# Sparse attention with a feed-forward block on one core: the first two tiles as a unit with separate up projections and a shared down projection

## Chip, cores and metric

The kernel runs on one core of one Trainium2 chip. The metric is the device time of one execution in microseconds (us). The kernel before has a median of 783.55 us over 3 runs.

## What is computed

For 4 batches, 8 heads, 768 positions and head size 64, attention runs with a mask over blocks of 32 positions; the 512 features of each position then go through a normalised two-layer feed-forward block (512 to 2048 to 512) with a residual:

```python
scores = np.matmul(q, k.transpose(0, 1, 3, 2)) / np.sqrt(D)
mask = np.abs(blk_i - blk_j) <= 1
mask = mask | (blk_i == 0) | (blk_j == 0) | (blk_i == 23) | (blk_j == 23)
for qb in range(24):
    for kb in sampled_blocks[qb]:          # three sampled blocks a row
        mask[qb*32:(qb+1)*32, kb*32:(kb+1)*32] = True
x = softmax(np.where(mask, scores, -1e9)) @ v    # heads side by side: (4, 768, 512)
xn = (x - mu) / np.sqrt(var + 1e-06) * g_ln
out = x + np.maximum(xn @ w_ch1, 0.0) @ w_ch2
```

## The kernel before

**Tiles, visits and jobs.** The 3072 positions are 24 tiles of 128, six a batch (`TORDER`). The attention of a tile is done in visits: two for an ordinary tile (jobs of kind N), five for the tile that holds the first and last blocks (kinds H and D). A job loads the keys and values that its visits share: on SyncE's (SP's) queue one large key load, twelve small ones of sampled blocks and the values, on GpSimd's (POOL's) queue gathers of sampled values. Two rooms for keys (`ks_s`) and two for values (`vs_s`) alternate, so a job's values wait until the visits two jobs back are through.

**A visit** passes from engine to engine: `scores` (L196; PE writes `ps`), `biggest` (L236; VectorE, DVE, writes `st`), `softmax` (L249; ScalarE, ACT, writes `p`), `turn` (L257; PE transposes into `pt`, ACT copies to SBUF), `attn_v` (L267; PE writes `pv`), `evict` (L300; DVE divides into `x`). Values of a visit come one step (`LAG`) after its scores. After the last visit of a tile `norm_a` (L334) makes the normalised fp16 halves `xh` (ACT) and `xl` (POOL), and `norm_b` (L347) transposes both with DMAs from SP's queue into `xth` and `xtl`.

**The feed-forward part** (`ffn`, L351) works on units. Before, the units are tile 0 alone, then pairs (1, 2), (3, 4) and so on, and tile 23 alone. The up projection makes, for each of 16 slices of 128 hidden features, 12 matmuls (three products of fp16 halves by four slices of the 512 features), with 128 columns for one tile and 256 for a pair; four slices of one tile, or two of a pair, fill a PSUM bank `pu`. ACT's relu (L377) makes the high half `hh`, DVE (L378) the low half `hl`. The down projection of a tile (`pd`, L392) is 48 matmuls of 512 columns; DVE adds the residual (L398) and POOL's queue stores it.

**The weights** come as 64-bit numbers and are split on the chip during the first steps. `split_w` (L418): three DVE operations (L421, L423, L425) rebuild a float, ACT makes the high half, and the low half is made by POOL for w1 (L435) and by DVE for w2 (`low_w2`, L444). w1 has eight pieces, two a step in steps 0 to 3; w2 has sixteen, four a step in steps 4 to 7, loaded on POOL's queue into four raw rooms. `con1` and `con2` are the rooms where the float stands. The raw rooms `raw2[0]` and `raw2[1]` are the second halves of `hh_s` and `hl_s`, which a pair needs and a single tile doesn't.

**What sets the order.** The program writes each engine's instructions in order of a loop over steps (L551); engines take their own in order and wait for each other by semaphores. In a step come scores, the values of the visit before, softmax, and then a list of tasks (loads, weight splits, `turn`, norms) with matmuls of the feed-forward part put between them by a budget (L576 to L600). The budget counts planned costs (84 for a matmul of 128 columns, 109 for 256, 215 in the down projection). A unit enters the queue at step `u.at` (L528), for tile 0 step 4, when all its tiles have been normalised. Between steps the generator stops where a weight piece that it needs has not been written in an earlier step.

Of the kernel before, what the change touches and what calls it, by code (L numbers as in the profile page):

```python
# [10 lines left out]
F16 = mybir.dt.float16  # L11
# [8 lines left out]
SW1 = 16.0  # L20
# [5 lines left out]
def sparse_attention_moe(  # L26
# [50 lines left out]
    hl_s = const.tile([P, FT * 2 * P], F16, name="hl")  # L77
    ot_s = ring("ot", 2, [P, DM], F32)
    stg = ring("stg", 2, [P, 2048], F16)
    id_sb = const.tile([P, P], F32, name="id_sb")  # L80
    g_sb = const.tile([P, DM], F32, name="g_sb")
    eps = const.tile([P, 1], F32, name="eps")

    nc.scalar.add_instruction(
# [2 lines left out]
        )  # L87
    )

    samp = const.tile([P, 2 * NB * NR], I32, name="samp")  # L90
    bid = const.tile([P, NB + 1], F32, name="bid")
    si = const.tile([P, NB, NR], I32, name="si")
    sf = const.tile([P, NB, NR], F32, name="sf")
    cf = const.tile([P, NB, NR], F32, name="cf")
    tf = const.tile([P, NB, NR], F32, name="tf")
    rf = const.tile([P, NB], F32, name="rf")
    rows = const.tile([P, NB], I32, name="rows")

# [201 lines left out]
    def evict(vi):  # L300
        n = 2 if vi.kind == "D" else 4
        u = vi.pv[:, 0 : n * 65].rearrange("p (h e) -> p h e", e=65)
        if vi.kind == "D":
            half = sm.tile([P, 2, 65], F32, tag="half", name=f"half{vi.i}")
# [44 lines left out]
        nc.sync.dma_start_transpose(out=xtl_s[t.u.i % 2][:, :, s], in_=xl_s[t.n % 2])  # L349

    def ffn(u):  # L351
        n = len(u.tiles) * P
        xth, xtl = xth_s[u.i % 2], xtl_s[u.i % 2]
        hh = hh_s[:, 0 : FT * n].rearrange("p (f n) -> p f n", n=n)
        hl = hl_s[:, 0 : FT * n].rearrange("p (f n) -> p f n", n=n)
        step = 512 // n
        c1 = 109 if n == 256 else 84
        for f in range(0, FT, step):
            while any((1, x // 2) not in split for x in range(f, f + step)):
                yield -1  # L360
            ph = ps_f.tile([P, 512], F32, tag="pf", name=f"pu{u.i}_{f}")
            for j in range(step):
                fs = slice((f + j) * P, (f + j + 1) * P)
                m = 0
                for w, x in ((w1h, xth), (w1l, xth), (w1h, xtl)):
                    for ct in range(CT):
                        nc.tensor.matmul(ph[:, j * n : (j + 1) * n], w[:, ct, fs], x[:, ct, 0:n],  # L367
                                         start=m == 0, stop=m == 3 * CT - 1,
                                         skip_group_check=True)
                        m += 1  # L370
                        if m < 3 * CT:
                            yield c1
                if j < step - 1:
                    yield c1
            dh = hh[:, f : f + step, :].rearrange("p f n -> p (f n)")
            dl = hl[:, f : f + step, :].rearrange("p f n -> p (f n)")
            nc.scalar.activation(dh, ph, AF.Relu)  # L377
            nc.vector.scalar_tensor_tensor(out=dl, in0=ph, scalar=0.0, in1=dh,  # L378
                                           op0=ALU.max, op1=ALU.subtract)
            if f + step == FT:  # L380
                u.up_done = True
            yield c1
        for t in u.tiles:

            ts = slice(t.pos * P, (t.pos + 1) * P)
            po = ps_f.tile([P, 512], F32, tag="pf", name=f"pd{t.n}")
            m = 0
            for f in range(FT):
                while split.get((2, f), s) >= s:
                    yield -1  # L390
                for x, w in ((hh, w2h), (hl, w2h), (hh, w2l)):
                    nc.tensor.matmul(po, x[:, f, ts], w[:, f, :], start=m == 0,  # L392
                                     stop=m == 3 * FT - 1)
                    m += 1
                    if m < 3 * FT:
                        yield 215
            ot = ot_s[t.n % 2]
            nc.vector.scalar_tensor_tensor(out=ot, in0=po, scalar=1.0 / (SW1 * SW2), in1=t.x,  # L398
                                           op0=ALU.mult, op1=ALU.add)
            nc.gpsimd.dma_start(out[t.b, t.t], ot)  # L400
            t.done = True
            yield 215

    split = {}
    late = [x[:, FT * P :] for x in (hh_s, hl_s)]
    w2f, w2g = (x.rearrange("p f e -> p (f e)") for x in (w2h, w2l))
    raw1 = [w2f[:, 0:4096], w2f[:, 4096:8192], w2g[:, 0:4096], w2g[:, 4096:8192]]
    con1 = [stg[0], stg[1], late[0], late[1]]
    raw2 = [late[0], late[1], stg[0], stg[1]]
    con2 = [x.bitcast(F16) for x in ot_s]  # L410

    def load_w1(i, dma):
# [47 lines left out]
                                         done=False, ready=False, normed=None, spread=None))  # L460
    n = 0
    while n < len(tiles):
        k = 1 if n == 0 or n == len(tiles) - 1 else 2
        u = SimpleNamespace(i=len(units), tiles=tiles[n : n + k], up_done=False, gen=None)
        for pos, t in enumerate(u.tiles):
            t.pos, t.u = pos, u
        units.append(u)
        n += k
# [56 lines left out]

    queue, nextu, s = [], 0, 0
    for u in units:
        u.at = max(FFN0, u.tiles[-1].visits[-1].i + LAG + 2)  # L528

    def run(amount):  # L530
        while queue and (amount > 0 or queue[0].left <= 0):
# [19 lines left out]
    while s < NV + LAG + 2 or queue or nextu < len(units):  # L551
# [102 lines left out]
```

## Time and profile before

| | us |
|---|---|
| median of 3 runs (783.39 to 784.59) | 783.55 |
| the profiled execution | 778.71 |
| its span, first to last instruction | 776.9 |
| PE busy / DVE busy / ACT busy / POOL busy in the span | 703.0 / 324.6 / 272.2 / 190.2 |
| PE busy from 143.70 to 204.00 (60.30 long) | 60.30 |
| mean granted clock of PE | 0.961 |

PE is the engine for matrix products, DVE and ACT work on elements, POOL also issues DMAs, SP only issues DMAs. Times in the text are counted from the first instruction of the profiled execution. A matmul's busy time overlaps that of the next; what one costs in a stream is the distance between starts. Tile names in a trace come without their numbers; a word ahead of the rows says which one it is.

### The profile page before, as it was taken

To read this page: it belongs to the slowest core of one execution; us is meant where nothing else is said; L and a number is where in the kernel's file an instruction comes from. 1 tells how busy PE (TensorE), PEld (TensorE's weight loads), DVE (VectorE), ACT (ScalarE), POOL (GpSimd) and SP (SyncE) were. 2 spreads that over 40 slices of the span, in tenths; PEclk is the share of its full clock that TensorE was granted. 3 is DMA by queue.
4 is the path that set the end of the run, shared out by engine and by line. 5 is a ranking of instruction groups with operands and counts; after the bars stand their busy time and mean duration, and the time that the engine had idled before them with its cause. 6 is when DMAs were issued, how large, how long until landed. Compare 5 with 4: busy or idle time off the path is not lost.

```text
span 776.9 us, 21816 instructions
## 1 busy us (share of the span) xinstructions
PE 703.0 (90%) x9344; PEld 475.4 (61%) x9344; DVE 324.6 (42%) x658; ACT 272.2 (35%) x561; POOL 190.2 (24%) x220
## 2 busy tenths in 40 slices
PE   0566475899999999999999999999999999999997
PEld 0234452675775774875875856765856857757764
DVE  2488889443351332443432323444331433432211
ACT  0357343344342332443341523344423423342200
POOL 5276414023312103113421103115221011210000
PEclk9956788899999999999999999999999999999999
DMA  8997887467948345569855437379864248531000
GB/s 329 287 321 207 285 291 211 115 181 204 258 112 206 92 145 159 150 179 246 234 156 132 129 128 211 119 180 270 215 168 131 61 151 219 148 88 27 14 29 14
DMA packets 109792, 132.16 MB, mean 170 GB/s; under 512 B 34560, under 2 KB 80896, under 8 KB 108672
## 3 DMA queue, kind: packets, MB, share of 16 engines
q1 hardware_dynamic: 96848, 83.92, 40.0%
q0 software_dynamic: 12416, 46.51, 18.2%
q8 instruction: 74, 1.21, 0.7%
q10 hardware_dynamic: 432, 0.34, 0.1%
q14 instruction: 22, 0.18, 0.1%
HBM read 118.15 MB, written 6.29 MB: 160 GB/s over the span
## 4 chain that ended last, share of the span: by engine, by line
PE 69%; issue 14%; DVE 8%; DMA 6%; POOL 1%; ACT 1%; SPq 0%; POOLq 0%; ACTq 0%; DVEq 0%
PE pu L367 27%; PE pd L392 25%; PE ps L203 6%; PE pv L274 6%; PE pt L264 5%; DMA ks<-kT 3%; DMA vs<-v 2%; DVE ot L423 1%; DVE w2l L445 1%; DVE ot L421 1%; DVE st L239 1%; DMA hl<-w 1%; DVE ot L425 1%; DMA samp<-sampled 0%; POOL xl L344 0%
## 5 line engine op out<-in xcount | busy, mean ns | idle before, releaser
L252 ACT ACTIVATE p<-ps,st 128x256 f32<-128x256 f32 (+1 forms) x208 | 85.7, 490 | 230.2 <-DVE rs L316 140.1
L367 PEld LDWEIGHTS <-w1h 128*128 128x128 f16 x1664 | 152.8, 98 | 18.6 <-issue 0.7
L392 PE MATMUL pd<-w2l,hh 128*128 128x512 f16 x384 | 146.5, 381 | 4.0 <-DVE w2l L445 4.0
L392 PE MATMUL pd<-w2h,hl 128*128 128x512 f16 x384 | 146.5, 382 | 0.0
L392 PE MATMUL pd<-w2h,hh 128*128 128x512 f16 x384 | 146.3, 381 | 0.0
L378 DVE SCALAR_TENSOR_TENSOR hl<-pu,hh 128x512 f16<-128x512 f32 x96 | 66.4, 691 | 174.1 <-ACT hh L377 173.7
L392 PEld LDWEIGHTS <-hh 128*128 128x128 f16 x768 | 74.8, 98 | 87.2 <-issue 4.3
L367 PE MATMUL pu<-xth,w1h 128*128 128x256 f16 (+1 forms) x832 | 120.4, 266 | 0.0
L367 PE MATMUL pu<-xth,w1l 128*128 128x256 f16 (+1 forms) x832 | 120.3, 266 | 0.0
L367 PE MATMUL pu<-xtl,w1h 128*128 128x256 f16 (+1 forms) x832 | 120.0, 265 | 0.0
L192 POOL DMA_INDIRECT vs<-v,rows x88 | 87.3, 992 | 88.0 <-PE pv L274 49.4
L239 DVE TENSOR_REDUCE st<-ps 128x4 f32<-128x1024 f32 (+1 forms) x60 | 69.0, 1150 | 93.7 <-PE ps L203 93.6
L203 PE MATMUL ps<-ks,q 64*32 64x256 f32 (+1 forms) x1664 | 75.7, 426 | 30.0 <-DMA ks<-kT 29.8
L377 ACT ACTIVATE hh<-pu 128x512 f16<-128x512 f32 x96 | 57.4, 598 | 118.0 <-PE pu L367 117.3
L264 PE MATMUL pt<-id_sb,p 128*128 128x128 f32 x448 | 66.8, 293 | 33.9 <-ACT p L252 33.9
L264 PEld LDWEIGHTS pt<-id_sb,p 128*128 128x128 f32 x448 | 55.0, 149 | 46.6 <-ACT p L252 40.4
L398 DVE SCALAR_TENSOR_TENSOR ot<-pd,x 128x512 f32<-128x512 f32 x24 | 16.6, 690 | 160.3 <-PE pd L392 160.3
L367 PEld LDWEIGHTS <-w1l 128*128 128x128 f16 x832 | 77.6, 98 | 8.5
L265 ACT COPY pt<-pt 128x512 f32<-128x512 f32 x120 | 61.9, 564 | 59.2 <-PE pt L264 58.5
L400 POOL DMA_DIRECT2D out<-ot x24 | 13.9, 580 | 257.1 <-DVE ot L398 257.1
L274 PEld LDWEIGHTS pv<-vs,pt 128*32 128x32 f32 x3584 | 56.4, 113 | 31.1 <-issue 23.7
L274 PE MATMUL pv<-vs,pt 128*32 128x65 f32 x3584 | 66.7, 227 | 0.7 <-ACT pt L265 0.6
(83 smaller groups left out, 414.8 us busy)
## 6 DMA issues: line engine op xcount, KB each, us to landing
ks<-kT SPq DMA_DIRECT2D x28, 768.0 KB, 5.1
ks<-kT SPq DMA_DIRECT2D x264, 64.0 KB, 4.1
vs<-v SPq DMA_DIRECT2D x20, 780.0 KB, 7.0
vs<-v SPq DMA_DIRECT2D x4, 1560.0 KB, 8.6
q<-qT SPq DMA_DIRECT2D x24, 256.0 KB, 3.4
out<-ot POOLq DMA_DIRECT2D x24, 256.0 KB, 3.3
vs<-v SPq DMA_DIRECT2D x16, 260.0 KB, 8.6
w2h<-w POOLq DMA_DIRECT2D x4, 1024.0 KB, 7.0
```

Source lines behind the costliest of these rows:

```text
L192: nc.gpsimd.indirect_dma_start(out=vs[:, 2 * gg, :], out_offset=None, in_=src, in_offset=bass.IndirectOffsetOnAxis(ap=rows[:, i : i + 1], ...
L203: nc.tensor.matmul(ps[32 * part : 32 * part + 32, col : col + n], lhs[64 * row : 64 * row + 64], rhs[64 * row : 64 * row + 64], start=True ...
L239: nc.vector.tensor_reduce(out=st[:, 0:n], in_=seen(vi), axis=AX.X, op=ALU.max, negate=True)
L252: nc.scalar.activation(p_s[:, h * w : (h + 1) * w], seen(vi)[:, h, :], AF.Exp, bias=vi.st[:, 4 + h : 5 + h], scale=0.125)
L264: nc.tensor.transpose(pt[:, k - lo, :], p_s[:, k * P : (k + 1) * P], id_sb)
L265: nc.scalar.copy(dst[:, lo:hi, :], pt[:, 0 : hi - lo, :])
L274: nc.tensor.matmul(pv[32 * row : 32 * row + 32, 65 * col : 65 * col + 65], pt[:, ch, 32 * row : 32 * row + 32], vs[:, vv, 65 * e : 65 * e ...
L367: nc.tensor.matmul(ph[:, j * n : (j + 1) * n], w[:, ct, fs], x[:, ct, 0:n], start=m == 0, stop=m == 3 * CT - 1, skip_group_check=True)
L377: nc.scalar.activation(dh, ph, AF.Relu)
L378: nc.vector.scalar_tensor_tensor(out=dl, in0=ph, scalar=0.0, in1=dh, op0=ALU.max, op1=ALU.subtract)
L392: nc.tensor.matmul(po, x[:, f, ts], w[:, f, :], start=m == 0, stop=m == 3 * FT - 1)
L398: nc.vector.scalar_tensor_tensor(out=ot, in0=po, scalar=1.0 / (SW1 * SW2), in1=t.x, op0=ALU.mult, op1=ALU.add)
```

## The change

Tiles 0 and 1 become one unit with a mark `apart`, tile 2 a unit of its own; from tile 3 on the pairs are the same as before. A unit that is apart enters the queue at step 3 as soon as its first tile has been normalised. Its up projections run one after the other, each with 128 columns, tile 1's result in the second half of `hh_s` and `hl_s`; its down projections run side by side, 3 matmuls of the one tile and 3 of the other for each slice of hidden features. The planned cost of a matmul of 128 columns is 62 instead of 84. Since the second halves are in use sooner, w2's raw rooms 0 and 1 move: one to the last quarter of `w2l`, one to a new room `room`, in which the index of the sampled blocks is made at the start. The half results of the D visits get two fixed rooms.

```diff
+    room = const.tile([P, 2048], F16, name="room")
+    half_s = ring("half", 2, [P, 2, 65], F32)
-    samp = const.tile([P, 2 * NB * NR], I32, name="samp")
+    part = room.bitcast(I32)
+    samp = part[:, 0 : 2 * NB * NR]
+    sf, cf, tf = (part[:, (2 + k) * NB * NR : (3 + k) * NB * NR].bitcast(F32)
+                  .rearrange("p (n r) -> p n r", r=NR) for k in range(3))
-    sf = const.tile([P, NB, NR], F32, name="sf")
-    cf = const.tile([P, NB, NR], F32, name="cf")
-    tf = const.tile([P, NB, NR], F32, name="tf")
...
     def ffn(u):
-        n = len(u.tiles) * P
...
+        groups = [[x] for x in u.tiles] if u.apart else [u.tiles]
+        for k, group in enumerate(groups):
+            n = len(group) * P
+            off = 0 if len(groups) == 1 else k * FT * P
+            while any(x.spread is None or x.spread >= s for x in group):
                 yield -1
+            hh = hh_s[:, off : off + FT * n].rearrange("p (f n) -> p f n", n=n)
+            hl = hl_s[:, off : off + FT * n].rearrange("p (f n) -> p f n", n=n)
+            cols = slice(group[0].pos * P, group[0].pos * P + n)
...
-        c1 = 109 if n == 256 else 84
+            c1 = 109 if n == 256 else 62
...
-        for t in u.tiles:
+        for group in [u.tiles] if u.apart else [[x] for x in u.tiles]:
+            po = [ps_f.tile([P, 512], F32, tag="pf", name=f"pd{x.n}") for x in group]
             for f in range(FT):
+
                 while split.get((2, f), s) >= s:
                     yield -1
-                for x, w in ((hh, w2h), (hl, w2h), (hh, w2l)):
...
+                for k, x in enumerate(group):
+                    for m, (y, w) in enumerate(((x.hh, w2h), (x.hl, w2h), (x.hh, w2l))):
...
-    raw2 = [late[0], late[1], stg[0], stg[1]]
+    raw2 = [w2g[:, 6144:8192], room, stg[0], stg[1]]
...
-        k = 1 if n == 0 or n == len(tiles) - 1 else 2
+        k = 1 if n == 2 or n == len(tiles) - 1 else 2
...
-        u.at = max(FFN0, u.tiles[-1].visits[-1].i + LAG + 2)
+        u.at = FFN0 if u.apart else u.tiles[-1].visits[-1].i + LAG + 2
...
-            if any(t.spread is None or t.spread >= s for t in u.tiles):
+            if any(t.spread is None or t.spread >= s for t in u.tiles[: 1 if u.apart else 2]):
...
-            u.left = 192 * (84, 109)[len(u.tiles) - 1] + 48 * 215 * len(u.tiles)
+            half = len(u.tiles) == 1 or u.apart
+            u.left = 192 * (62 * len(u.tiles) if half else 109) + 48 * 215 * len(u.tiles)
```

What this moves on the engines shows at three places. In the rows `ps3` belongs to visit 3, `pv2` to visit 2, `pt3` to visit 3; `pu0_4` is the bank of tile 0's slices 4 to 7.

PE, from the scores of visit 3 on. Before:

```order
L203 MATMUL ps3_531<-ks1_80,q1_89 32x256 x16
L274 MATMUL pv2_551<-vs1_84,pt0_86 32x65 x32
L264 MATMUL pt3_0_592<-id_sb_110,p_85 128x128 x4
L264 MATMUL pt3_4_598<-id_sb_110,p_85 128x128 x4
L203 MATMUL ps4_620<-ks0_79,q0_88 32x256 x16
L274 MATMUL pv3_640<-vs1_84,pt1_87 32x65 x32
L367 LDWEIGHTS w1h_75
L367 MATMUL pu0_0_681<-xth0_100,w1h_75 128x128
```

Now, with the repeated pairs of weight load and matmul left out (pu0_0 has 48, and 16 of pu0_4 stand ahead of the turn of visit 3):

```order
L206 MATMUL ps3_530<-ks1_80,q1_89 32x256 x16
L277 MATMUL pv2_550<-vs1_84,pt0_86 32x65 x32
L376 LDWEIGHTS w1h_75
L376 MATMUL pu0_0_591<-xth0_100,w1h_75 128x128
...
L376 MATMUL pu0_4_655<-xth0_100,w1h_75 128x128
L267 MATMUL pt3_0_672<-id_sb_111,p_85 128x128 x4
L267 MATMUL pt3_4_678<-id_sb_111,p_85 128x128 x4
```

The first up projection has moved ahead of the turn of visit 3; the scores of visit 4 now follow 144 up matmuls, and the last 48 of tile 0 stand behind the values of visit 3.

DVE, at the same place, between the last operation on w1 and the first on w2. Before:

```order
L425 SCALAR_TENSOR_TENSOR hl_105<-w2l_78,hl_105 128x1024
L239 TENSOR_REDUCE st4_637<-ps4_620 128x4
L240 TENSOR_SCALAR st4_637<-st4_637 128x4
L316 TENSOR_SCALAR rs3_673<-pv3_640 128x4
L318 RECIPROCAL rs3_673<-rs3_673 128x4
L322 TENSOR_TENSOR x1_91<-pv3_640,rs3_673 128x256
L378 SCALAR_TENSOR_TENSOR hl_105<-pu0_0_681,hh_104 128x512
L421 TENSOR_SCALAR ot0_106<-hh_104 128x512
```

Now:

```order
L436 SCALAR_TENSOR_TENSOR hl_105<-w2l_78,hl_105 128x1024
L387 SCALAR_TENSOR_TENSOR hl_105<-pu0_0_591,hh_104 128x512
L387 SCALAR_TENSOR_TENSOR hl_105<-pu0_4_655,hh_104 128x512
L387 SCALAR_TENSOR_TENSOR hl_105<-pu0_8_720,hh_104 128x512
L242 TENSOR_REDUCE st4_789<-ps4_772 128x4
L243 TENSOR_SCALAR st4_789<-st4_789 128x4
L319 TENSOR_SCALAR rs3_825<-pv3_792 128x4
L321 RECIPROCAL rs3_825<-rs3_825 128x4
L325 TENSOR_TENSOR x1_91<-pv3_792,rs3_825 128x256
L387 SCALAR_TENSOR_TENSOR hl_105<-pu0_12_833,hh_104 128x512
L432 TENSOR_SCALAR ot0_106<-w2l_78 128x512
```

All four low halves of tile 0 stand ahead of the first operation on w2 (the last row), three of them ahead of visit 4's maximum; before, one stood there.

ACT, during the second step of w2 (`w2h` from `ot0` or `ot1` is the high part of a piece, pieces 4 to 7 here). Before:

```order
L431 ACTIVATE w2h_77<-ot0_106 128x512
L377 ACTIVATE hh_104<-pu0_4_771 128x512
L431 ACTIVATE w2h_77<-ot1_107 128x512
L265 COPY pt1_87<-pt5_0_949 128x512
L265 COPY pt1_87<-pt5_4_955 128x512
L431 ACTIVATE w2h_77<-ot0_106 128x512
L431 ACTIVATE w2h_77<-ot1_107 128x512
L377 ACTIVATE hh_104<-pu0_8_923 128x512
```

Now:

```order
L442 ACTIVATE w2h_77<-ot0_106 128x512
L386 ACTIVATE hh_104<-pu1_0_1018 128x512
L442 ACTIVATE w2h_77<-ot1_107 128x512
L268 COPY pt1_87<-pt5_0_1109 128x512
L268 COPY pt1_87<-pt5_4_1115 128x512
L386 ACTIVATE hh_104<-pu1_4_1075 128x512
L442 ACTIVATE w2h_77<-ot0_106 128x512
L442 ACTIVATE w2h_77<-ot1_107 128x512
L386 ACTIVATE hh_104<-pu1_8_1144 128x512
```

Tile 1's first bank (`pu1_0`) stands where tile 0's second stood, and a further relu (`pu1_4`) stands behind the copies of visit 5; the low halves on DVE stand in the same places between the pieces. On SP and POOL the order of loads is the same; on POOL the stores of tiles 0 and 1 now follow each other.

## Rows read from the trace of the kernel before

**Rows 1.** The page, busy tenths in 40 slices of the span (19.4 us each).
```profile
PE   0566475899999999999999999999999999999997
...
DVE  2488889443351332443432323444331433432211
```

**Rows 2.** Busy time by stretch; columns: stretch, length, busy time (instructions) of each engine, granted clock, DMA, GB/s.
```profile
94.60:99.30 4.70, 4.67 (x36) 4.52 (x37) 4.05 (x7) 2.18 (x5) 1.32 (x2) 0.51 0.55 115
...
143.70:204.00 60.30, 60.30 (x924) 40.99 (x922) 24.95 (x57) 22.64 (x49) 14.92 (x18) 1.00 0.62 169
...
304.00:404.00 100.00, 100.00 (x1440) 70.26 (x1438) 41.33 (x91) 38.14 (x84) 27.96 (x32) 1.00 0.71 196
```

**Rows 3.** Timeline of PE; columns: start, us, engine, line, operation, out<-in, size, count [idle before].
```profile
75.50 0.39 PE L367 MATMUL pu<-xth,w1l 128*128 128x128 f16 x4
...
76.84 0.39 PE L367 MATMUL pu<-xth,w1l 128*128 128x128 f16 x4
...
97.35 0.63 PE L367 MATMUL pu<-xth,w1l 128*128 128x128 f16 x4
97.78 0.63 PE L367 MATMUL pu<-xtl,w1h 128*128 128x128 f16 x4
```

**Rows 4.** Chain that ended last, in order of time; columns: start, us, what.
```profile
203.99 4.47 PE pu L367 x40
209.34 6.11 PE pu L367 x56
...
248.99 6.91 PE pd L392 x32
```

**Rows 5.** Timeline of PE, values of visit 2 and turn of visit 3.
```profile
58.37 1.12 PE L274 MATMUL pv<-vs,pt 128*32 128x65 f32 x64
66.14 1.97 PE L264 MATMUL pt<-id_sb,p 128*128 128x128 f32 x8 [6.65 <-ACT p L252]
```

**Rows 6.** Timeline of SP, transposes of tile 0; the last row: DMA issues, median us to landing.
```profile
69.70 1.30 SPq L348 DMA_TRANSPOSE xth<-xh  x1
71.10 1.20 SPq L349 DMA_TRANSPOSE xtl<-xl  x1
...
xtl<-xl SPq DMA_TRANSPOSE x24, 2.9
```

**Rows 7.** Timeline of DVE, first operation on w2.
```profile
81.27 0.46 DVE L421 TENSOR_SCALAR ot<-hh 128x512 int32<-128x512 int32 x1 [0.91 <-DMA hh<-w]
```

**Rows 8.** Timeline of ACT (three rows), then of DVE, pieces 4 to 8 of w2.
```profile
93.52 0.62 ACT L343 CAST xh<-xn 128x512 f16<-128x512 f32 x1
...
100.80 0.63 ACT L431 ACTIVATE w2h<-ot 128x512 f16<-128x512 f32 x1 [2.55 <-DVE ot L425]
101.34 1.05 ACT L265 COPY pt<-pt 128x512 f32<-128x512 f32 x2
...
98.29 0.69 DVE L378 SCALAR_TENSOR_TENSOR hl<-pu,hh 128x512 f16<-128x512 f32 x1 [0.58 <-ACT hh L377]
...
101.40 0.43 DVE L421 TENSOR_SCALAR ot<-stg 128x512 int32<-128x512 int32 x1
...
111.81 0.42 DVE L421 TENSOR_SCALAR ot<-hh 128x512 int32<-128x512 int32 x1
```

**Rows 9.** Timeline of PE, turn of visit 8.
```profile
139.63 1.54 PE L264 MATMUL pt<-id_sb,p 128*128 128x128 f32 x6 [4.60 <-ACT p L252]
```

**Rows 10.** Timeline of SP, loads for visits 13 to 16 and transposes of tiles 3 and 4.
```profile
166.33 0.33 SPq L180 DMA_DIRECT2D vs<-v  x1
...
183.43 0.42 SPq L144 DMA_DIRECT2D ks<-kT  x1
185.71 0.34 SPq L180 DMA_DIRECT2D vs<-v  x1
...
198.05 1.21 SPq L349 DMA_TRANSPOSE xtl<-xl  x1
```

**Rows 11.** The page, costliest groups: busy us, mean ns of one.
```profile
L367 PEld LDWEIGHTS <-w1h 128*128 128x128 f16 x1664 | 152.8, 98 | 18.6 <-issue 0.7
```

More of the change, by code (lines that the diff above doesn't have):

```diff
@@ L303, in evict @@
         if vi.kind == "D":
-            half = sm.tile([P, 2, 65], F32, tag="half", name=f"half{vi.i}")
+            half = half_s[vi.r % 2]
             if not vi.r:
@@ L351, in ffn @@
     def ffn(u):
-        n = len(u.tiles) * P
         xth, xtl = xth_s[u.i % 2], xtl_s[u.i % 2]
-        hh = hh_s[:, 0 : FT * n].rearrange("p (f n) -> p f n", n=n)
-        hl = hl_s[:, 0 : FT * n].rearrange("p (f n) -> p f n", n=n)
-        step = 512 // n
-        c1 = 109 if n == 256 else 84
-        for f in range(0, FT, step):
-            while any((1, x // 2) not in split for x in range(f, f + step)):
-                yield -1
[L361 to L382, printed above, removed]
@@ L383, in ffn @@
-        for t in u.tiles:
-            ts = slice(t.pos * P, (t.pos + 1) * P)
-            po = ps_f.tile([P, 512], F32, tag="pf", name=f"pd{t.n}")
-            m = 0
+        groups = [[x] for x in u.tiles] if u.apart else [u.tiles]
[3 more added lines that the diff above has]
+            while any(x.spread is None or x.spread >= s for x in group):
+                yield -1
+            hh = hh_s[:, off : off + FT * n].rearrange("p (f n) -> p f n", n=n)
+            hl = hl_s[:, off : off + FT * n].rearrange("p (f n) -> p f n", n=n)
+            cols = slice(group[0].pos * P, group[0].pos * P + n)
+            step = 512 // n
+            c1 = 109 if n == 256 else 62
+            for f in range(0, FT, step):
+                while any((1, x // 2) not in split for x in range(f, f + step)):
+                    yield -1
+                ph = ps_f.tile([P, 512], F32, tag="pf", name=f"pu{group[0].n}_{f}")
+                for j in range(step):
+                    fs = slice((f + j) * P, (f + j + 1) * P)
+                    m = 0
+                    for w, x in ((w1h, xth), (w1l, xth), (w1h, xtl)):
+                        for ct in range(CT):
+                            nc.tensor.matmul(ph[:, j * n : (j + 1) * n], w[:, ct, fs],
+                                             x[:, ct, cols], start=m == 0, stop=m == 3 * CT - 1,
+                                             skip_group_check=True)
+                            m += 1
+                            if m < 3 * CT:
+                                yield c1
+                    if j < step - 1:
+                        yield c1
+                dh = hh[:, f : f + step, :].rearrange("p f n -> p (f n)")
+                dl = hl[:, f : f + step, :].rearrange("p f n -> p (f n)")
+                nc.scalar.activation(dh, ph, AF.Relu)
+                nc.vector.scalar_tensor_tensor(out=dl, in0=ph, scalar=0.0, in1=dh,
+                                               op0=ALU.max, op1=ALU.subtract)
+                if f + step == FT and k == len(groups) - 1:
+                    u.up_done = True
+                yield c1
+            for x in group:
+                x.hh, x.hl = hh, hl
+                x.ts = slice(0, P) if u.apart else slice(x.pos * P, (x.pos + 1) * P)
@@ L390, in ffn @@
                     yield -1
-                for x, w in ((hh, w2h), (hl, w2h), (hh, w2l)):
[L392 to L395, printed above, removed]
-                        yield 215
[L397 to L402, printed above, removed]
+                for k, x in enumerate(group):
+                    for m, (y, w) in enumerate(((x.hh, w2h), (x.hl, w2h), (x.hh, w2l))):
+                        end = f == FT - 1 and m == 2
+                        nc.tensor.matmul(po[k], y[:, f, x.ts], w[:, f, :],
+                                         start=f == 0 and m == 0, stop=end)
+                        if end:
+                            ot = ot_s[x.n % 2]
+                            nc.vector.scalar_tensor_tensor(out=ot, in0=po[k],
+                                                           scalar=1.0 / (SW1 * SW2), in1=x.x,
+                                                           op0=ALU.mult, op1=ALU.add)
+                            nc.gpsimd.dma_start(out[x.b, x.t], ot)
+                            x.done = True
+                        yield 215
     split = {}
@@ L462, in sparse_attention_moe @@
     while n < len(tiles):
-        k = 1 if n == 0 or n == len(tiles) - 1 else 2
-        u = SimpleNamespace(i=len(units), tiles=tiles[n : n + k], up_done=False, gen=None)
+        k = 1 if n == 2 or n == len(tiles) - 1 else 2
+        u = SimpleNamespace(i=len(units), tiles=tiles[n : n + k], up_done=False, gen=None,
+                            apart=n == 0)
         for pos, t in enumerate(u.tiles):
```

## Prediction

> **What bounds the kernel now.** I read the page's forty slices first [rows 1]: TensorE (PE) is busy to nine tenths from the ninth slice on, and less in the eight before it; there VectorE (DVE) shows eights and a nine, in the slices three to seven, while weights are split. So the run has two stages with different limits. The busy times by stretch [rows 2] put the border: from 143.70 to 204.00 PE is busy for all of 60.30 us, and so in every stretch up to the last (304 to 404 stands for them). After about 140 us the time is PE's list of work; before it, the chain of waits runs through DVE, which turns 64-bit weights into pairs of fp16 (eight pieces of w1, sixteen of w2), and PE fills in. The order of PE's work is the same in both kernels from visit 15 on: there stands the first up projection of tiles 3 and 4, at 203.99 [rows 4]. **The change is worth what it moves that point by**, and nothing later can give it back, since PE has no idle time behind it.
>
> Two things decide it: how late the split of w2 ends, and how much PE work (or other work) is left then.
>
> **Term 1: a first stop, ahead of w2.** The first up projection (pu0_0) now stands on PE directly behind the weighted values of visit 2, which end at 58.37 + 1.12 = 59.5; before, the turn of visit 3 stood there, at 66.14 [rows 5]. pu0_0 needs the transposed halves of tile 0. SyncE (SP) issues them at 69.70 and 71.10, behind the keys, in both kernels; the second half takes 2.9 us to land [rows 6], so 74.0. Eight matmuls run on the first half, 40 wait. PE has been idle for over ten us and runs at its lower clock: after such a pause the granted clock of 94.60 to 99.30 is 0.51, that is 1.2 GHz [rows 2], and four matmuls of 128 columns take 0.43 us; at 2.4 GHz 24 take 76.84 - 75.50 = 1.34, so 0.056 each [rows 3]. 40 x 0.107 = 4.3, to 78.3. Then 16 more at 0.056 (0.9), the turn of visit 3 (8 transposes, 1.97 at the lower clock [rows 5], so 1.0), 80 up matmuls (4.5), scores and values of visits 4 and 3 (some 2.1, by the 1.12 of [rows 5]), the last 48 (2.7): 89.5. ScalarE's (ACT) relu takes about 0.63 (an equal pass over 512 columns) and DVE's low half 0.69 [rows 8]: 90.8. All of this is ahead of DVE's first piece of w2, which began at 81.27 [rows 7]. **9.5 us late**; 7.5 if the clock were full at once (40 x 0.051 less).
>
> **Term 2: a second stop, between w2's pieces 4 and 5.** There DVE now takes the low half of tile 1's first up projection; before, that of tile 0's second, long computed. Tile 1's fp16 half came 94.14 - 81.27 = 12.9 us after DVE's first w2 piece [rows 7, 8]: now 103.7. Its second transpose goes out 1.4 later and lands after 2.9 [rows 6]: 108.0; 40 matmuls at the lower clock, 112.3; relu and low half, 113.6. Piece 5 began at 98.29 + 0.69 = 98.98 [rows 8], so **14.6 late** in all. Then comes one low half more than before, ahead of piece 6. On ACT its relu stands behind the high part of piece 5 and two copies of visit 5: 101.43 - 98.98 = 2.45 after piece 5's start, plus 1.05, plus 0.63 and 0.69, makes 4.8; piece 6 began 101.40 - 98.98 = 2.4 after it [rows 8]. **2.4 more: 17.0.** With a full clock in both stops 12.9. From the higher end I take off 0.7 a stop, since PE will be some 4 us into its work when the last of the 40 run: 15.5. From piece 8 on (111.81 [rows 8]) the DVE rows are the same ones in both kernels, so the turn of visit 8, at 139.63 [rows 9], comes at 155.1.
>
> **Term 3: what PE has left then.** Before, from 139.63 to 203.99: 64.4 us. Tiles 1 and 2 went up as a pair, 192 matmuls of 256 columns at 0.109; now tile 2 alone, 192 of 128 at 0.056 [rows 3, 4]: 10.2 less. Of down matmuls 101 were left (5 and 96); now 23 and tile 2's 48, 30 fewer at 0.216 [rows 4]: 6.5 less. **64.4 - 16.7 = 47.7.** The other 192 up matmuls added (tile 1 by itself) lie in PE's idle time before 140, as do 73 down matmuls (15.8 us): from the end of tile 1's up work, at some 123 (111.6, 144 matmuls at 0.056 and two visits' 3), PE has 32 us for them and three visits' 6 us. Their cost is nothing as long as that holds.
>
> **Term 4: SP is late next.** The queue's order is unchanged, but PE now needs its loads sooner. SP is held by the values' room until visit 10 is through (the issue at 166.33), then issues that job, loads and transposes, and is ready for the next job at 183.85, 17.5 us later; from that issue (185.71) to tile 4's second transpose (198.05) are 12.3 [rows 10], and 2.9 to land. That is 32.7 us from visit 10 to the point where the up projection of tiles 3 and 4 can run. Before, PE took 203.99 - 166.33 = 37.7, and SP waited 1.9 for it. Now visit 10 ends 26.7 - 148 x 0.109 + 97 x 0.056 + 18 x 0.216 = 19.9 after the turn of visit 8 (matmuls counted in the two orders), and 52.6 would be the end of SP's chain, against PE's own 47.7. The wait is nowhere in the trace of before; its bounds are 47.7 (SP in time) and 53. I take 51.5, nearer to SP's measured length, less a microsecond because eight matmuls run ahead on the first half.
>
> **Sum.** 155.1 + 51.5 = 206.6 against 203.99: 2.6 us later. The profiled execution took 778.71, so 781.3; it lies 4.8 below the median of the runs, 783.55, and I forecast **786.2** for that. The bounds: 139.63 + 12.9 + 47.7 = 200.2 (3.8 earlier) and 139.63 + 17.0 + 53 = 209.6 (5.6 later).
>
> What costs nothing: the index's new place (the same instructions, at the start of the program, long before w2 is loaded); w2's two moved raw rooms, as all four loads still stand on POOL behind the last w1 subtraction; the two output stores, now back to back; the fixed rooms for half results.
>
> **Rivals.** *SP does not bind.* Its issues are paced by the landing of earlier loads, which may be quicker; then PE's 47.7 stands, 155.1 + 47.7 = 202.8, 1.2 earlier: no change. With the stops at 14.2 (midway to their lower bound) it is 201.5, 2.5 earlier and 781.1, **faster**. It decides at tile 4's transpose landing within 47.7 of visit 8's turn. For it speaks that SP had 1.9 us to spare; against it, that 32.7 is measured and nothing on SP is removed. Chance 0.30, a little over half of it faster.
>
> *PE falls behind under the split.* The turn of visit 6 now has 22 down matmuls ahead of it (4.8 us), and ACT's next piece of w2 stands behind its copies. By my times it is about 1.5 us late; what of that reaches DVE adds to the sum: 787.7. Chance 0.13.
>
> *Weight loads set the pace at 128 columns.* A weight load is busy for 98 ns [rows 11]; if it did not overlap, tile 2's 192 would cost 192 x 0.042 = 8.1 more, PE's 47.7 become 55.8, and the run 790.5. The rows speak against it: 24 pairs of load and matmul pass in 1.34 us [rows 3]. Chance 0.04. The Trainium skill speaks against the change here: "TensorE: Matmul & The Clock Gate", section "Back-to-back issue gap", gives about 81 ns sustained for pairs of weight load and matmul at 128 columns, and says the shorter gap of an isolated matmul leaves out the weight load. By it (an estimate from that page) tile 2 would cost 4.8 more, nearly all of it behind SP's chain, and the run about 787; this trace does not agree, with 56 ns a pair.
>
> That the down projections don't really move is excluded by the order: 73 of 96 stand ahead of visit 8's turn.
>
> **How the numbers follow.** The forecast case has 0.53; in 0.07 of that the stops come out a microsecond and a half shorter, which is no change. 0.2% is 1.6 us, about what the runs can tell (they spread over 1.2). Faster 0.16 (SP in time and short stops). Same 0.14 + 0.07 = 0.21. Slower 0.46 + 0.13 + 0.04 = 0.63. The likeliest case alone spans 784.5 to 788.5; the range runs from 779.8, the lower bound of the sum (783.55 - 3.8), to 790.5, past its upper bound (789.2) to the last rival.
>
> **What would show it.** In the profile after: DVE's first w2 operation near 91 instead of 81.27, idle before it and released by ACT's relu; a second idle time of some 5 us ahead of tile 1's first low half; visit 8's turn near 155; PE waiting for SP's loads (keys at visits 13 and 15, or a transpose) between 185 and 207, where it had no idle time before; the up projection of tiles 3 and 4 near 206.6, and equal stretches after it. If visit 8's turn comes before 153, the stops are mis-sized; if PE shows no wait for loads, term 4 falls and the result is no change or better.

## The result: 1.2% slower, and what the profile after shows

The changed kernel has a median of 792.87 us (791.93 to 793.80, 4 runs), the kernel before 783.52 in the same comparison: a ratio of 1.0117, 95% interval 1.0104 to 1.0130, 9.35 us slower. The forecast was 786.2 with a range up to 790.5. The sign was right; the time lies 2.4 us past the range.

| us | before | after | forecast |
|---|---|---|---|
| DVE, first operation on w2 | 81.27 | 90.14 | 90.8 |
| turn of visit 8 | 139.63 | 154.79 | 155.1 |
| visit 10's end (value load issued) | 166.33 | 174.43 | 175.0 |
| up projection of tiles 3 and 4 | 203.99 | 213.66 | 206.6 |
| span of the profiled execution | 776.9 | 790.2 | |

The forecast holds up to visit 10 and fails behind it. The page of the changed kernel, busy tenths in slices of 19.8 us, to be laid beside [rows 1]: PE has a four in the eighth slice (138 to 158) and a seven in the eleventh (198 to 217), where it had an eight and a nine.

```profile
PE   0464669499799999999999999999999999999997
...
DVE  2487668754233242343351423443432433442211
```

The two stops. DVE's timeline after (start, us, engine, line, operation, tiles, size, idle time and its releaser): the low half of tile 0's last bank, the first operation on w2, the low half of tile 1's first bank, piece 8.

```profile
89.53 0.69 DVE L387 SCALAR_TENSOR_TENSOR hl<-pu,hh 128x512 f16<-128x512 f32 x1 [2.98 <-ACT hh L386]
90.14 0.46 DVE L432 TENSOR_SCALAR ot<-w2l 128x512 int32<-128x512 int32 x1
...
111.30 0.69 DVE L387 SCALAR_TENSOR_TENSOR hl<-pu,hh 128x512 f16<-128x512 f32 x1 [5.07 <-ACT hh L386]
...
126.95 0.42 DVE L432 TENSOR_SCALAR ot<-w2l 128x512 int32<-128x512 int32 x1
```

PE's timeline at the same places, and the turn of visit 8:

```profile
72.06 0.59 PE L376 MATMUL pu<-xth,w1h 128*128 128x128 f16 x4 [10.61 <-DMA xth<-xh]
...
105.14 0.58 PE L376 MATMUL pu<-xth,w1h 128*128 128x128 f16 x4 [13.32 <-DMA xth<-xh]
...
154.79 1.54 PE L267 MATMUL pt<-id_sb,p 128*128 128x128 f32 x6 [9.17 <-ACT p L255]
```

PE stands for 10.61 and 13.32 us at a transpose, DVE behind it. Piece 8 is 15.14 us later than in [rows 8], the turn of visit 8 is 15.16 later than in [rows 9].

Where it went wrong. SP's timeline after: the value load behind visit 10, then the value load, the twelve key loads and the transposes of the next job, which are the rows of [rows 10].

```profile
174.43 0.33 SPq L183 DMA_DIRECT2D vs<-v  x1
...
192.17 0.45 SPq L183 DMA_DIRECT2D vs<-v  x1
...
195.87 12.38 SPq L156 DMA_DIRECT2D ks<-kT  x12
208.35 1.21 SPq L351 DMA_TRANSPOSE xth<-xh  x1
209.65 1.21 SPq L352 DMA_TRANSPOSE xtl<-xl  x1
```

From 174.43 to 192.17 are 17.74 us (17.5 forecast), but from there to the second transpose 17.48, not 12.3. The twelve key loads take 12.38; the list of SP's waits (us in total, times, longest) for 195 to 210 says why:

```profile
SPq L156 <- DMA vs<-v: 6.1, 2, 5.7
```

SP stops at the seventh key load, the eighth DMA behind the value load of 192.17, from 199.01 to 204.89, until that load has landed, 12.7 us after its issue. In the kernel before, the same list has no such row at this place: there the seventh key load went out at 193.68 without a wait, so the value load of 185.71 had landed by then, in at most 8.0 us. SP's timeline at the seventh key load, after and before:

```profile
204.89 0.33 SPq L156 DMA_DIRECT2D ks<-kT  x1
```

```profile
193.68 0.33 SPq L153 DMA_DIRECT2D ks<-kT  x1
```

PE's timeline shows what hangs on it (scores of visit 15 in three pieces, values of visit 14, up projection of tiles 3 and 4):

```profile
206.67 1.35 PE L206 MATMUL ps<-ks,q 64*32 64x256 f32 x8 [3.60 <-DMA ks<-kT]
208.26 1.06 PE L206 MATMUL ps<-ks,q 64*32 64x256 f32 x4 [0.23 <-DMA ks<-kT]
209.91 1.92 PE L206 MATMUL ps<-ks,q 64*32 64x256 f32 x20 [0.59 <-DMA ks<-kT]
211.76 1.96 PE L277 MATMUL pv<-vs,pt 128*32 128x65 f32 x64
213.66 1.03 PE L376 MATMUL pu<-xth,w1h 128*128 128x256 f16 x4
```

The waits are for keys; none for a transpose shows. Behind the 3.60 us without work the clock has fallen. Two stretches of the changed kernel (columns as in [rows 2]); the second has a granted clock of 0.50, 1.2 GHz, and the values take 1.96 us instead of 1.12 [rows 5]:

```profile
143.70:204.00 60.30, 48.62 (x815) 31.40 (x813) 32.02 (x73) 24.58 (x54) 17.42 (x20) 0.92 0.77 204
...
206.00:212.00 6.00, 4.50 (x43) 1.54 (x47) 0.13 (x1) 0.00 (x0) 0.00 (x0) 0.50 0.47 115
```

In the first of them PE was busy for all of 60.30 us before [rows 2], now for 48.62.

Why did the same load take longer? POOL's timeline, first of the kernel before, then of the changed one, with the first gather of visits 15 and 16 last:

```profile
188.67 0.58 POOL L400 DMA_DIRECT2D out<-ot  x1 [5.00 <-DVE ot L398]
189.56 1.38 POOL L192 DMA_INDIRECT vs<-v,rows  x1 [0.30 <-PE pt L264]
```

```profile
189.63 1.17 POOL L171 COPY ks<-kg 128x512 f32<-128x512 f32 x2 [5.34 <-DMA kg<-kT]
190.95 0.99 POOL L195 DMA_INDIRECT vs<-v,rows  x1 [0.16 <-PE pv L277]
```

Before, tile 1's output store stands on POOL ahead of the gathers and waits for DVE's residual; the four gathers start 3.85 us after the value load's issue (185.71). Now both stores of the first unit are long gone, and the gathers start 1.2 us ahead of it.

### The profile page after: what moved, and what is told of

Read it like the earlier page. It is cut to its first block, busy times and chain, and to the rows that moved or that the text cites. A ratio compares the mean times of both kernels' runs of the same rounds, so it can differ in the third digit from the quotient of the medians.

```text
span 790.2 us, 22200 instructions
## 1 busy us (share of the span) xinstructions
PE 704.3 (89%) x9536; PEld 478.1 (61%) x9536; DVE 323.4 (41%) x658; ACT 272.0 (34%) x561; POOL 189.5 (24%) x220
## 3 DMA queue, kind: packets, MB, share of 16 engines
q1 hardware_dynamic: 96848, 83.92, 39.4%
## 4 chain that ended last, share of the span: by engine, by line
PE 66%; issue 14%; DMA 9%; DVE 6%; SPq 2%; ACT 1%; POOL 1%; POOLq 0%; DVEq 0%; ACTq 0%
PE pu L376 27%; PE pd L404 22%; PE pv L277 6%; DMA vs<-v 6%; PE ps L206 6%; PE pt L267 5%; SPq L156 2%; DMA ks<-kT 2%; DVE ot L434 1%; DVE w2l L456 1%; DVE ot L432 1%; DMA xtl<-xl 1%; DVE ot L436 1%; DVE st L242 1%; DMA room<-sampled 1%
## 5 line engine op out<-in xcount | busy, mean ns | idle before, releaser
L376 PEld LDWEIGHTS <-w1h 128*128 128x128 f16 x1792 | 157.7, 99 | 42.0 <-issue 25.0
L376 PE MATMUL pu<-xth,w1h 128*128 128x256 f16 (+1 forms) x896 | 124.8, 261 | 24.7 <-DMA xth<-xh 23.9
L376 PE MATMUL pu<-xth,w1l 128*128 128x256 f16 (+1 forms) x896 | 124.2, 260 | 0.0
L376 PE MATMUL pu<-xtl,w1h 128*128 128x256 f16 (+1 forms) x896 | 123.4, 260 | 0.6 <-DMA xtl<-xl 0.6
L376 PEld LDWEIGHTS <-w1l 128*128 128x128 f16 x896 | 81.3, 100 | 8.7 <-issue 0.8
L267 PE MATMUL pt<-id_sb,p 128*128 128x128 f32 x448 | 65.2, 286 | 18.0 <-ACT p L255 18.0
L267 PEld LDWEIGHTS pt<-id_sb,p 128*128 128x128 f32 x448 | 52.9, 145 | 29.7 <-ACT p L255 23.6
```

Of the source, the lines that this page charges most:

```text
L267: nc.tensor.transpose(pt[:, k - lo, :], p_s[:, k * P : (k + 1) * P], id_sb)
```

## Experiments

Theory A: the point that decides is set by SP's chain, which visit 10's end starts and which is some 39 us long because the value load lands late beside the gathers. Rivals: full DMA engines whatever the order (B, C; F in the run with the down projections one by one), the loads binding in the kernel before as well (D), PE's own work (E). Positions in us, read from each profile; the time against the kernel before on the same chip, single executions marked *. The experiments ran on three chips, on which the median of the kernel before is 779.74, 780.60 and 782.98.

| kernel | first w2 op | turn of visit 8 | visit 10's end | up proj. 3, 4 | from visit 10 | time / before |
|---|---|---|---|---|---|---|
| before | 81.27 | 139.63 | 166.33 | 203.99 | 37.7 | 1 |
| after | 90.14 | 154.79 | 174.43 | 213.66 | 39.2 | 1.0117 |
| values of visits 15, 16 last | 90.64 | 155.68 | 175.96 | 213.63 | 37.7 | 1.0135 [1.0111, 1.0158] |
| their gathers left out | 91.43 | 155.49 | 176.52 | 210.40 | 33.9 | 786.29 / 779.74* |
| their gathers last | 91.68 | 156.71 | 176.68 | 213.66 | 37.0 | 789.06 / 780.60* |
| unit at step 4 | 83.59 | 147.04 | 166.69 | 205.43 | 38.7 | 1.0011 [0.9999, 1.0023] |
| second stop off | 90.87 | 153.26 | 173.28 | 212.64 | 39.4 | 788.72 / 779.74* |
| downs one by one | 90.24 | 155.06 | 180.12 | 219.10 | 39.0 | 796.58 / 782.98* |

**Values last.**

```diff
                 pre += [(next, (gen, 0)), (values, (nxt,))] + [(next, (gen, 0))] * 6
+                if nxt.i == 7:
+                    pre.append(pre.pop(-7))
```

> The changed kernel, in which the values and gathers of the job for visits 15 and 16 are issued behind its twelve small key loads instead of ahead of them. Theory A (SP's key loads are held for 5.9 us from 199.01 because the value load issued at 192.17 takes 12.7 us to land while four gathers of POOL run beside it, and PE at visit 15 waits for these keys): the twelve keys go out in one piece, PE's 4.4 us of waits ahead of the scores of visit 15 and the lower clock behind them go, the up projection of tiles 3 and 4 starts at 203 to 207 instead of 213.66, and the run is 7 to 10 us faster than the change (783 to 786). Rival B (the DMA engines are simply full from 192 to 204, and whatever is last in the queue lands at the same time): PE waits as long as before, for keys or for values, the up projection stays within 2 us of 213.66, the time within 2 us of 792.9.

Measured 1.0135 of the kernel before (the changed kernel: 1.0117): no gain. The wait for keys is gone, as A said, but another stands in its place. PE's timeline, and from the list of DMA issues (195 to 214) the median time to landing:

```profile
205.32 1.11 PE L277 MATMUL pv<-vs,pt 128*32 128x65 f32 x64
213.63 1.01 PE L376 MATMUL pu<-xth,w1h 128*128 128x256 f16 x4 [7.20 <-DMA xth<-xh]
```

```profile
xth<-xh SPq DMA_TRANSPOSE x1, 9.8
```

The transposes are issued 4.5 us earlier but now queue behind the value load, and the first lands after 9.8 us; in the kernel before it took 4.4. That they stand behind the large load is one reason that fits; but in the same list POOL's store took 9.6 and its gathers 9.1 (4.8 and 5.0 in the kernel before), so this run does not tell the order of SP's queue from DMA engines that are full for all. B's time came true, with the wait at the transposes instead of the keys or values.

**Gathers left out, gathers last** (the first leaves out the sampled values of visits 15 and 16, so its output differs; in the second the gathers are a function of their own, which `values` no longer calls for this job).

```diff
-        for gg, i in enumerate(job.blocks):
+        for gg, i in enumerate(job.blocks if job.i != 7 else []):
```

```diff
         tasks.append((norms, ()))
+        if vi and nxt and nxt.i == 7:
+            tasks.append((gathers, (nxt,)))
```

> The changed kernel without the four gathers of sampled values for visits 15 and 16 (these values are left out). Theory A: the value load of that job lands some 7 us after its issue, as in the kernel before, instead of 12.7; SP's stop among the key loads shrinks from 5.9 to at most 1.5 us; the up projection of tiles 3 and 4 comes at 205 to 209. Rival B: the stop stays above 4 us and the up projection within 2 us of 213.66.

> The changed kernel with only the four gathers for visits 15 and 16 moved, on POOL, behind the norms at the end of their step; the value load stays where it is. In the kernel before, tile 1's output store stands ahead of these gathers and holds them until 3.85 us after the value load's issue; in the changed kernel that store is long gone and the gathers start 1.2 us ahead of it. Theory A (this order is why the value load lands in 12.7 us instead of 7.2, and SP stops for 5.9 us): the stop falls to 1 to 2.5 us, and the up projection of tiles 3 and 4 comes at 207 to 210.5, as without the gathers (210.40). Rival B (only the bytes of the gathers count, not their place): the stop stays above 4 us, the up projection at 212 or later.

SP's waits from 195 to 210, without the gathers and then with them last:

```profile
SPq L156 <- DMA vs<-v: 2.2, 2, 1.4
```

```profile
SPq L156 <- DMA vs<-v: 2.1, 2, 1.4
```

Both fall from 6.1 to 2.2 and 2.1. With the gathers last, the seventh key load went out at 202.32:

```profile
202.32 0.33 SPq L156 DMA_DIRECT2D ks<-kT  x1
```

The value load, issued at 194.01, had then landed in 8.3 us (8.2 without the gathers) instead of 12.7: the place of the gathers ahead of the value load, not the load itself, made the long stop. (The "7.2" of the expectations was misread; the bound is 8.0, as above.) The Trainium skill, "DMA: Bandwidth & Descriptors", section "Queues, rings and completion order", says that a DMA engine with work from several queues serves them in turn, packet by packet, and that one queue's descriptors are taken in order; these two runs agree with the first. The 9.8 us of the transposes fit the second, but do not show it, as POOL's transfers were slow then too. At the up projection A was wrong: 210.40 lies past its 205 to 209, and 213.66 is where B had put it. Counted from visit 10's end, which came 2 us later in both runs, 5.3 us without the gathers but only 2.2 with them last, where the last keys still land late (scores at 209.32 behind a wait of 2.01) and the clock is low. So the place of the gathers explains SP's stop, but only 2 of the 5 us that they cost PE; how the rest comes about, no run takes apart.

**Unit at step 4; second stop off.**

```diff
-    NX, LAG, FFN0 = 5, 1, 3
+    NX, LAG, FFN0 = 5, 1, 4
```

```diff
-            while any(x.spread is None or x.spread >= s for x in group):
+            while any(x.spread is None or x.spread >= s - k for x in group):
```

> The changed kernel with the first unit entering at step 4, as tile 0 did before, so that the first up projection no longer stands ahead of the turn of visit 3. If the first stop cost what the trace says (DVE's first operation on w2 at 90.14 instead of 81.27), that operation comes at 82 to 84.5 and the turn of visit 8 at 145 to 149 instead of 154.79; the second stop is left. With what then stands between that turn and the up projection of tiles 3 and 4 (47.7 us of PE, 52.6 of SP with prompt loads, 58.9 as the changed kernel had it) the latter starts at 198 to 207, and the run is 6 to 14 us faster than the change: 779 to 787. If the lateness is not the stop's (the two low halves ahead of w2, or the order of ACT), the first w2 operation stays above 87 and the run above 788.

> The changed kernel with only the second stop taken away: tile 1's up projection may start one step later, step 6. Theory: DVE's first w2 operation stays at 90, but from piece 4 to piece 8 DVE has no idle time above 2 us, the turn of visit 8 comes at 149 to 152 instead of 154.79, and the up projection of tiles 3 and 4 at 204 to 210. If PE cannot make up 192 up matmuls and 73 down matmuls in steps 6 and 7, the turns of visits 6 to 8 show PE without idle time and the turn of visit 8 stays at 153 or later.

With the unit at step 4 the first stop is gone, as expected: 83.59 and 147.04, and visit 10 ends as early as in the kernel before. Yet the run is level with it, 1.0011. SP's waits (185 to 202) and PE's timeline:

```profile
SPq L156 <- DMA vs<-v: 6.7, 2, 6.5
```

```profile
199.11 1.36 PE L206 MATMUL ps<-ks,q 64*32 64x256 f32 x8 [4.00 <-DMA ks<-kT]
...
205.43 0.61 PE L376 MATMUL pu<-xth,w1h 128*128 128x256 f16 x4
```

38.7 us behind visit 10 again. The work that PE saved is waited away. The second stop alone is not worth the 3 to 6 us that I gave it: the turn of visit 8 came 1.5 us earlier (153.26), and the up projection at 212.64, not at 204 to 210. Moved to step 6, the up projection of tile 1 holds DVE there, ahead of piece 8:

```profile
118.13 0.69 DVE L387 SCALAR_TENSOR_TENSOR hl<-pu,hh 128x512 f16<-128x512 f32 x1 [1.54 <-ACT hh L386]
120.11 0.69 DVE L387 SCALAR_TENSOR_TENSOR hl<-pu,hh 128x512 f16<-128x512 f32 x1 [1.29 <-ACT hh L386]
123.67 0.69 DVE L387 SCALAR_TENSOR_TENSOR hl<-pu,hh 128x512 f16<-128x512 f32 x1 [2.87 <-ACT hh L386]
```

**Downs one by one.**

```diff
-        for group in [u.tiles] if u.apart else [[x] for x in u.tiles]:
+        for group in [[x] for x in u.tiles]:
```

> The changed kernel with the down projections of tiles 0 and 1 one after the other instead of side by side. Counted in the two orders, 32 more down matmuls (6.9 us at 0.216) stand between the turn of visit 8 and the up projection of tiles 3 and 4, and 3.2 us more of PE's work ahead of visit 10's end. Theory A (SP's chain, held by visit 10's end and 39.2 us long, sets that point; PE's work has 11 us to spare): the turn of visit 8 stays at 154 to 156, the up projection moves by these 3.2 alone, to 216 to 218, and down matmuls behind visit 10 fill PE's waits. Rival E (PE's work sets it): it moves by 6.9, to 220 or later. Rival F (the point hangs on the DMA engines alone): it stays at 213 to 214.5.

Visit 10 ended 5.7 us later, not 3.2, and the up projection came at 219.10, past A's 216 to 218 and short of E's 220; F's 213 to 214.5 is out. It is 39.0 us behind visit 10's end, so the chain's length held. Of the 2.5 us that visit 10 was later than counted, some 1.7 are gaps without a releaser in its own values, of a kind that the last section shows:

```profile
178.34 0.33 PE L277 MATMUL pv<-vs,pt 128*32 128x65 f32 x6 [0.41 <-issue]
179.11 0.31 PE L277 MATMUL pv<-vs,pt 128*32 128x65 f32 x3 [0.44 <-issue]
```

219.10 alone would hardly tell A from E. Against E speaks that PE waited 2.6 us for keys ahead of it here, and 4.8 us in the changed kernel. What the side-by-side order is worth is not shown more closely than by this one execution.

**All value loads behind the norms**, in the changed kernel, with the unit at step 4, and in the kernel before:

```diff
-                pre += [(next, (gen, 0)), (values, (nxt,))] + [(next, (gen, 0))] * 6
+                pre += [(next, (gen, 0))] * 7
...
         tasks.append((norms, ()))
+        if vi and nxt:
+            tasks.append((values, (nxt,)))
```

> The changed kernel with value loads and gathers of every job moved behind the norms at the end of their step, so that on SP neither keys nor transposes stand behind a value load. Theory A: SP is then no longer held by visit 10, PE has no wait for keys or transposes at visit 15, and the up projection of tiles 3 and 4 stands where PE's own work puts it, 47.7 us behind the turn of visit 8: 202 to 204.5; the run is 8 to 12 us faster than the change, level with the kernel before. Rival C (the DMA engines are full, so that keys or transposes are late anyway): 207 or later, less than 6 us gained.

> Unit entered at step 4, and all value loads and gathers behind the norms. Theory A: the turn of visit 8 at 146 to 148.5 as with step 4 alone, the up projection of tiles 3 and 4 some 48 us later, 194 to 198 (205.43 with step 4 alone): 7 to 10 us faster than that kernel and 6 to 10 faster than the kernel before. Rival C: the loads still set the point, 200 or later, at most 5 us faster than before.

> The kernel before with all value loads and gathers behind the norms. Theory A: there PE's own list of work sets the up projection of tiles 3 and 4, not the loads, so this point stays within 1 us of 203.99 and the time within 2 us. Rival D (the loads set it in the kernel before too): the point comes 2 us or more earlier.

Now SP's chain no longer starts at visit 10's end. The up projection of tiles 3 and 4 in the changed kernel, and with the unit at step 4:

```profile
204.32 0.61 PE L376 MATMUL pu<-xth,w1h 128*128 128x256 f16 x4
```

```profile
197.92 0.61 PE L376 MATMUL pu<-xth,w1h 128*128 128x256 f16 x4
```

Both as A said. The turns of visit 8 stand at 153.08 and 146.82, so 51.2 and 51.1 us lie between, of which 2.2 each are waits for keys: PE's own part is about 48.9. So DMA engines that are full whatever the order (C) don't hold the point. In the kernel before it came at 202.71, 1.3 earlier, past A's 1 and short of D's 2, and the time stayed (1.0013, 0.9999 to 1.0027). As PE had no idle time there from 143.70 to 204.00 [rows 2], PE sets the point, and D falls. The times of the first two fell short of the expectations, 1.0045 (1.0028 to 1.0062) and 0.9982 (0.9963 to 1.0002) of the kernel before (in time the first gained less than C's 6 us), since moving all jobs loses again later. Against the profile of the kernel before, the kernel with the unit at step 4 is 5.5 us ahead at visit 28 and 1.3 at visit 46. PE's timeline from visit 44 on:

```profile
538.11 0.60 PE L376 MATMUL pu<-xtl,w1h 128*128 128x256 f16 x4 [0.37 <-DMA xtl<-xl]
543.41 0.28 PE L376 MATMUL pu<-xth,w1l 128*128 128x256 f16 x1 [2.63 <-issue]
```

**The early jobs alone, and without the second stop.** As above, with `nxt.i <= 7` as the condition.

> Unit entered at step 4, value loads and gathers behind the norms for the jobs up to visits 15 and 16 alone, so that the later stage keeps its order. Theory A: the up projection of tiles 3 and 4 at 196 to 199, as when all jobs were moved (197.92), and no loss behind it (there 5.9 us were lost between visits 29 and 46): 5 to 9 us faster than the kernel before. If the losses behind visit 29 come from elsewhere, 0 to 3 us faster.

> The same, and tile 1's up projection may start only at step 6, so that neither stop is left. Theory A: the turn of visit 8 at 141 to 145 (146 to 148.5 with the second stop), the up projection of tiles 3 and 4 at 192 to 196, a further 2 to 5 us faster. If PE cannot make up the work moved into steps 6 and 7, the turn of visit 8 is not earlier than with the second stop and the time equal.

Both beat both kernels: 0.9953 (0.9940 to 0.9966) with the unit at step 4, and 0.9967 (0.9956 to 0.9978) without the second stop. The intervals overlap; by its median the first is the fastest found, 3.5 us below the kernel before. It came short of 5 to 9, and the second was hardly earlier at visit 8 (146.26 against 146.95, not 141 to 145). The up projection of tiles 3 and 4 came at 202.49 and 201.58, not at 196 to 199 and 192 to 196; behind it the first loses nothing (575.5 us to the end, as with the rooms alone, below). PE's timeline of the first has two waits that the changed kernel lacks:

```profile
142.53 1.53 PE L277 MATMUL pv<-vs,pt 128*32 128x65 f32 x48 [7.46 <-DMA vs<-v]
...
194.59 0.22 PE L277 MATMUL pv<-vs,pt 128*32 128x65 f32 x1 [1.11 <-issue]
```

The value load of visits 7 to 10, now late, holds PE just ahead of visit 8's turn in both (7.46 and 5.36 us), so what the second stop is worth can't be read here. And in both 4.2 us in eight pieces are lost in the values of visits 12 and 13, most of them in visit 13, to nothing that the profile shows.

**Rooms alone.** The kernel before with w2's raw rooms, the index and the half results moved:

```diff
-    raw2 = [late[0], late[1], stg[0], stg[1]]
+    raw2 = [w2g[:, 6144:8192], room, stg[0], stg[1]]
```

> The kernel before with only the rooms moved: w2's two raw rooms, the index made in one of them, the two fixed rooms of half results. All theories: nothing waits for these rooms, so DVE's first operation on w2 stays within 0.5 us of 81.27, the turn of visit 8 within 1 of 139.63, the time within 1.5 us of the kernel before. If a room did cost something, the first w2 operation would come later.

The time is the same, 1.0002 (0.9993 to 1.0011). The first operation on w2 came at 83.08, behind 1.55 us of idle time for its raw load, and the turn of visit 8 at 141.05, both later than I allowed; part of it lies ahead of w2 (visit 4's maximum at 74.08 instead of 73.48). The up projection of tiles 3 and 4 came at 206.95, 3.0 later than in the profile of before, though the kernels are equally fast on this chip. There is no profile of the kernel before from this chip, so positions of profiles from different chips can be compared to some 3 us only; the length from visit 10's end (38.3 against 37.7) differs less.

## Why the prediction was wrong

- **Term 1** held, 90.14 against 90.8, partly by luck. The second half had landed by 73.33, not at 74.0, and from 75.83 on four up matmuls took 0.22 us instead of 0.43, inside the 40 that I had all at the lower clock. So the first bank was through at 76.7 instead of 78.3; then PE lost 0.73 us to no releaser (up matmul at 86.20), which took back half.
- **Term 2** held: 15.2 us at the turn of visit 8 against 15.5; the stop ahead of piece 5 was 12.9 late instead of 14.6, most of which the 0.7 taken off for each stop covers. PE did not fall behind; that rival is out.
- **Term 3** was right in kind and about 1 us small: some 48.9 us of PE's own work where the loads are out of the way (the two runs with all value loads behind the norms) against 47.7. Weight loads don't set the pace: in the changed kernel tile 2's pairs start at 181.56 and, twelve later, at 182.23, 0.056 each, as in [rows 3] and not the 0.081 of the Trainium skill's "TensorE: Matmul & The Clock Gate", section "Back-to-back issue gap".
- **Term 4 is the step that failed**, in its size. That SP's chain binds was right, and PE waited for keys at visits 13 and 15 as said; the transposes, which I took for the chain's end, were not what it waited for. Its 51.5 us measured 58.9. Visit 10 ended 19.6 us after visit 8's turn (19.9) and the first job's loads took 17.7 (17.5). The failure is "from that issue (185.71) to tile 4's second transpose (198.05) are 12.3": 17.5, 5.2 more, since I took the landing of the value load to be the same: it took 12.7 us instead of at most 8.0. The last piece, 2.9 less 1.0, measured 4.0: PE had been waiting for keys, and the scores of visit 15 and the values of visit 14 still ran behind the last of them at half the clock. 5.2 + 2.1 + 0.2 - 0.3 = 7.2, and 213.66 - 206.6 = 7.1.
- **The step behind it** is the sentence "What costs nothing: ... the two output stores, now back to back". I looked at what waits for them, not at what they had been holding: POOL's four gathers, 3.85 us behind the value load. The run with the gathers last shows that their place is 4 of the 6 us of SP's stop. Their place does not account for the whole error: from visit 10's end to the point I forecast 31.6 us (175.0 to 206.6); the changed kernel took 39.2, with the gathers last 37.0, without them 33.9. So the gathers are some 5 of these 7.6 us, their place about 2, by one execution each; the rest is open.
- **The bound** was too low for the same reason: 53 was SP's measured length, not a length at another state of the DMA engines.
- **The profile and the median.** 213.66 is 9.7 us late and the medians differ by 9.35, but that they agree so closely is partly chance. The spans differ by 13.3: besides 1.1 at low clock in the first up matmuls, the changed kernel's profile loses 1.2 us each at the values of visits 28 and 43, which the profile of before does not. The kernel with the rooms alone, as fast as before, has them too (from visit 28's to visit 29's maximum 11.4 us, in the profile of before 10.2), so they are not the change's, and they are part of why the profile of before lay 4.8 below its median. Against the rooms alone, 213.66 is 6.7 late and the span (790.2 against 782.4) 7.8 longer: the point and the low clock behind it. So at the least 6.7 of the 9.35 hang on this point.

## What to carry to other kernels

A change that takes work from one engine is worth what the next chain leaves of it; measure that chain from the event that starts it (here a room that visit 10 sets free, 39 us ahead), and count the landing times in it as prices that hold for the order of transfers in which they were read. When an instruction leaves a queue, ask not only who waited for it but what it kept back: here a store held four gathers behind a load, and without it the load took 12.7 us to land instead of at most 8.0. A wait that is moved rather than removed (values behind keys, keys behind values) shows up at the next consumer; what helped was to issue the load that nobody needs soon behind the transposes, and only in the stage where it hurts.

## What was not expected of the hardware

PE loses time in the values' matmuls to no releaser in the profile. Changed kernel, values of visits 28 and 43:

```profile
376.40 1.08 PE L277 MATMUL pv<-vs,pt 128*32 128x65 f32 x58 [0.49 <-issue]
...
546.36 1.02 PE L277 MATMUL pv<-vs,pt 128*32 128x65 f32 x53 [0.50 <-issue]
```

The profiles of the four kernels that ran on one chip (rooms, downs one by one, the two early ones) have such gaps at both visits; the other eight experiments' profiles, from two other chips, have neither, those of two kernels nearly like the changed one (values last, gathers left out) among them. In 20 us around the two gaps (364 to 384 and 544 to 564) the mean busy share of the DMA engines is 0.86 and 0.89; in the kernel before it is 0.97 and 0.99 at about the same visits (364 to 384 and 524 to 544), without a gap, so full engines alone don't decide it. The cause stays open.
